# Whole-array products for the first attention groups, and the conversion's shifted words in one PSUM bank

## The chip, the cores and the metric

The kernel runs on one core of one Trainium2 chip. The metric is the device time of one execution in microseconds (us). Engines: PE (TensorE), DVE (VectorE), ACT (ScalarE), POOL (GpSimd), and SP, which here only issues DMAs. Matrix products take their operands from SBUF and write to PSUM, which has eight banks; a bank holds 512 fp32 words per partition.

## The reference

Windowed attention, then two feed-forward stages on its output. q and k are drawn with larger factors than v; the weights w1, w2, w3, w_out, w_in and w_out2 are float64.

```python
def _attn_ref(q, k, v):                       # (4, 8, 576, 64)
    window = 64
    scores = 1.0 / np.sqrt(D) * np.matmul(q, k.transpose(0, 1, 3, 2))
    rel = pos[:, None] - pos[None, :]
    scores = np.where((rel >= 0) & (rel < window), scores, -1000000000.0)
    scores = scores - np.max(scores, axis=-1, keepdims=True)
    attn = np.exp(scores)
    attn = attn / (np.sum(attn, axis=-1, keepdims=True) + 1e-09)
    return np.matmul(attn, v)

def _moe_ref(x, w1, w2, w3, w_out):           # x: 2304 x 512, d_ff 1024
    return ((x @ w1) * (x @ w2) @ w3) @ w_out

def _moe2_ref(x, w_in, w_out):                # d_ff 2048
    h = x @ w_in
    return (h * (1.0 / (1.0 + np.exp(-h)))) @ w_out
```

## The kernel before

**Weights.** They come as 64-bit words and are made into fp32 on the chip, 72 chunks of 128x512. A chunk (class `Chunk`) is loaded by SP (`words`), then ACT takes the scaled upper halves into `cv_b` and the lower halves into `cv_r` (L106, L107), DVE shifts `cv_b` by three bits in place (L115, `fraction`), DVE puts the sign bit of the upper half back (L118, `sign`, inputs `words` and `cv_b`), and POOL adds the rounded lower half (L122). Most chunks are then split into a high and a low part for three-pass products: ACT makes the high part (L130), DVE or POOL the low part (L134). `steps_to` runs this as a pipeline of chunk steps; the DVE steps of a chunk wait in `parts` and are put between the attention's DVE steps by `fill`.

**Attention.** 72 groups g of 128 queries and two heads. The first 17 (`PLAIN`) are computed in plain fp32, whose product of one instruction in the program is two records on PE; the others with split operands. `half` 2g transposes the probabilities of group g-1 (L286), computes the scores of g (L242; on 64 rows of the array, one product a head) and lets DVE reduce them with the mask (L253) and ACT exponentiate them; half 2g+1 normalises (L272, L274, L276 on DVE) and computes the values of g-1 (L311 and L312; each head in its own 64 columns of the array), which ACT copies out (L313).

**Stages.** The W stage (`phase_w`) multiplies w3 with w_out (L451, `accw`, in plain fp32), with 28 of the halves and the first conversions between its products. Then six blocks of phase A follow (`phase_a`, L479 and L499), which carry the other halves; block 0 has the rest of the first conversions, the last block those of w_in and w_out2 (`hooks5`). The last stage computes `h` (L601), its gate (ACT L606, DVE L607, ACT and POOL L79, L82) and `o` (L620), and the last conversions run on into its first rows. All instructions stand in the order in which the code issues them; each engine and SP works its list off in that order and waits at semaphores.

**PSUM.** Pool `ps` has four banks under one tag that rotate for the sums accw, ab, x and h; `psa` has one bank for scores, one for transposes and two for values.

Of the kernel before, what the change touches and what calls it, by code (L numbers as in the profile page):

```python
# [22 lines left out]
NB = 384  # L23
# [18 lines left out]
@with_exitstack  # L42
def tile_window_attention_ffn(ctx, tc, qkv, mask, ident, w1, w2, w3t, w_out, w_in, w_out2, out):

# [7 lines left out]
    main = ctx.enter_context(tc.tile_pool(name="main", bufs=1))  # L52
    ps = ctx.enter_context(tc.tile_pool(name="ps", bufs=4, space=PSUM))
    dram = ctx.enter_context(tc.tile_pool(name="dram", bufs=1, space=DRAM))
# [21 lines left out]
    def split(hi, lo, src, eng_hi, eng_lo):  # L76
# [7 lines left out]
        )  # L84

    PASSES = ((0, 0), (0, 1), (1, 0))


    class Chunk:
# [19 lines left out]
        def stage1(self):  # L109


            b = self.b

            def fraction():
                nc.vector.tensor_scalar(out=b, in0=b, scalar1=3, scalar2=None, op0=ALU.logical_shift_left)  # L115

            def sign():
                nc.vector.scalar_tensor_tensor(  # L118
                    out=b, in0=self.high, scalar=-0x80000000, in1=b, op0=ALU.bitwise_and, op1=ALU.bitwise_or
                )  # L120
# [62 lines left out]
    sm = [att.tile([128, 2, 192], F32, name=f"sm{i}", tag=f"sm{i}", bufs=1) for i in range(2)]  # L183
    k_lo = [att.tile([128, 384], F32R, name=f"klo{i}", tag=f"klo{i}", bufs=1) for i in range(2)]
    HEADS = (0, slice(0, 64)), (1, slice(64, 128))
    xhl = {}
# [12 lines left out]
    def load_qk(g):  # L199
        if g < NG and g not in loaded:  # L200
            loaded.add(g)
            qk_raw[g] = att.tile([128, 768], F32, name=f"qk{g}", tag="qk", bufs=2)
            u, c = place(g)
            p, f = (slice(0, 64), slice(128, 768)) if plain(g) else (slice(0, 128), slice(0, 768))
            nc.sync.dma_start(out=qk_raw[g][p, f], in_=qkv[u, c, p, f])

    def load_v(g):
        if g < NG and ("v", g) not in loaded:
            loaded.add(("v", g))
            v_raw[g] = att.tile([128, 3, 64], F32, name=f"v{g}", tag="v", bufs=3)  # L210
            u, c = place(g)
            nc.sync.dma_start(out=v_raw[g].rearrange("p t d -> p (t d)"), in_=qkv[u, c, :, 768:960])
# [23 lines left out]
    def scores(g):  # L236
        s_ps = psa.tile([128, 2, 192], F32, name=f"s{g}", tag="s")
        t = qk_raw.pop(g) if plain(g) else qk_st.pop(g)
        n = 64 if plain(g) else 128
        for h in range(2):  # L240

            nc.tensor.matmul(  # L242
                s_ps[:, h], lhsT=t[0:n, 128 + h * 128 : 256 + h * 128], rhs=t[0:n, 384 + h * 192 : 576 + h * 192],
                start=(h == 0), stop=(plain(g) and h == 1),
            )
        if not plain(g):
            nc.tensor.matmul(s_ps, lhsT=t[:, 0:128], rhs=k_lo[g % 2], start=False, stop=True)  # L247
# [128 lines left out]
    def phase_w():  # L376
# [36 lines left out]
        ready += [W12_B + 24 + (4 if W12_B == 16 else 0)] * 2  # L413

        loads_to(2)
        load_qk(0)
# [9 lines left out]
        load_v(2)  # L426
        for t in k_lo:
            for h, hs in HEADS:
                nc.gpsimd.memset(f32(t[hs, 192 - h * 192 : 384 - h * 192]), 0.0)
        steps_to(ready[0])  # L430
# [4 lines left out]
        for s in range(16):  # L435
            sw, j = divmod(s, 8)
            loads_to(ready[s + 2] + (3 if s > 1 else 0))
            if j == 0:
                for i in range(4):
                    acc[i] = ps.tile([128, 512], F32, name=f"accw{sw}_{i}", tag="ps")  # L440
            for part in range(2):
# [19 lines left out]
    def phase_a(blk, hooks):  # L461
# [9 lines left out]
        for s in range(16):  # L471
            f, m = divmod(s, 2)
            unit(s)
            fs = slice((f % 4) * 128, (f % 4 + 1) * 128)
            acc = ps.tile([128, NB], F32, name=f"ab{blk}_{s}", tag="ps")
            for k in range(4):
# [12 lines left out]
        for o in range(4):  # L489
            acc = ps.tile([128, NB], F32, name=f"x2_{blk}_{o}", tag="ps")  # L490
            for f in range(8):
# [25 lines left out]
    with tc.manual_schedule():  # L517
# [4 lines left out]
        for blk in range(1, NBLK - 1):  # L522
            phase_a(blk, lambda n: None)
        late.close()


# [67 lines left out]
        def emit_h(j, f):  # L594
            x = x2t[j]
            n = x.shape[-1]
            acc = ps.tile([128, n], F32, name=f"h{j}_{f}", tag="ps")
            fs = slice((f % 4) * 128, (f % 4 + 1) * 128)
# [73 lines left out]


def masks():

# [38 lines left out]
```

## Time and profile before

| | us |
|---|---|
| median of 3 runs (lowest to highest) | 904.78 (904.33 to 905.51) |
| the profiled execution | 904.8 |
| its span, first to last instruction | 903.0 |
| busy: PE, DVE, ACT, POOL | 877.2, 517.6, 492.0, 437.4 |

The profiled execution has a time of its own, and its span leaves out what lies before its first and behind its last instruction. Busy times are sums over the whole span. PE is the busiest engine in all stages, and DVE is close to full in two of them only: up to some 110 us (W stage) and from some 460 to 570 us (last conversions). What a shorter DVE or PE step is worth must be read from these stages.

### The profile page before, as it was taken

Reading aid. Unit: us, or ns where it says so; the run is one execution under the profiler, and the core shown is the slowest. Engines: PE = TensorE matmul, PEld = TensorE weight load, DVE = VectorE, ACT = ScalarE, POOL = GpSimd, SP = SyncE. Lnnn points to the kernel's source line nnn. Section 1 sums busy time; section 2 is a strip of 40 time slices with the busy share of each in tenths; the row PEclk is TensorE's granted clock in tenths of the full one; section 3 lists DMA queues with packets and bytes.
Section 4 is the critical chain, followed back from the end, with each engine's and each line's share of the span. In section 5 each row is a group of like instructions: output and inputs, shape, how many; then the busy total and the mean of one; then the engine's idle time right before and its main releaser. Section 6 shows DMA issues by size and latency. Waiting matters only on the chain.

```text
span 903.0 us, 13301 instructions
## 1 busy us (share of the span) xinstructions
PE 877.2 (97%) x4430; PEld 741.9 (82%) x4430; DVE 517.6 (57%) x1202; ACT 492.0 (54%) x1219; POOL 437.4 (48%) x470
## 2 busy tenths in 40 slices
PE   5999899999999999999999999999999999999998
PEld 2444378999999999999998776788888888888896
DVE  6989777888888878878488899311111111111111
ACT  6676577787788778787475775322222222222222
POOL 4557546556555566456297668422322232223222
PEclk9999899999999999999999999999999999999999
DMA  8866413332333322431567500110011000100100
GB/s 291 282 220 225 121 51 95 113 114 89 115 101 106 115 97 89 125 109 49 187 227 275 221 0 1 48 47 0 1 47 47 1 0 24 47 1 0 48 1 24
DMA packets 39396, 84.71 MB, mean 94 GB/s; under 512 B 4320, under 2 KB 17632, under 8 KB 39328
## 3 DMA queue, kind: packets, MB, share of 16 engines
q1 hardware_dynamic: 33280, 74.43, 25.2%
q10 hardware_dynamic: 6048, 9.44, 2.8%
q8 instruction: 35, 0.57, 0.3%
q14 instruction: 33, 0.27, 0.1%
HBM read 74.42 MB, written 9.44 MB: 93 GB/s over the span
## 4 chain that ended last, share of the span: by engine, by line
PE 78%; DVE 9%; POOL 4%; DMA 4%; issue 3%; ACT 2%; SPq 1%; POOLq 0%; DVEq 0%; ACTq 0%
PE o L620 18%; PE h L601 18%; PE ab L479 18%; PE x L499 10%; DVE cv_b L115 3%; PE accw L451 3%; PE t L286 2%; DVE cv_b L118 2%; PE s L242 2%; PE o L318 2%; DVE hl L134 1%; POOL cv_b L122 1%; PE s L247 1%; DMA qk<-in_qkv 1%; PE o L319 1%
## 5 line engine op out<-in xcount | busy, mean ns | idle before, releaser
L620 PE MATMUL o<-hl,g 128*128 128x512 f32 x864 | 213.0, 392 | 4.1 <-POOL g L82 3.6
L601 PE MATMUL h<-x2t,hl 128*128 128x512 f32 (+1 forms) x960 | 213.4, 371 | 0.0
L82 POOL TENSOR_TENSOR g<-sg,g 128x512 fp32r<-128x512 f32 (+1 forms) x80 | 96.0, 1200 | 241.9 <-ACT g L79 227.4
L607 DVE TENSOR_TENSOR sg<-h,sg 128x512 f32<-128x512 f32 (+1 forms) x80 | 51.0, 637 | 279.7 <-ACT sg L606 279.7
L601 PEld LDWEIGHTS h<-x2t,hl 128*128 128x128 f32 x960 | 169.4, 188 | 33.9
L620 PEld LDWEIGHTS o<-hl,g 128*128 128x128 f32 x864 | 160.3, 188 | 42.0 <-POOL g L82 6.8
L606 ACT ACTIVATE sg<-h 128x512 f32<-128x512 f32 (+1 forms) x80 | 44.2, 553 | 187.7 <-PE h L601 187.7
L479 PE MATMUL ab<-xa,hl 128*128 128x384 f32 x576 | 116.6, 337 | 0.0
L479 PE MATMUL ab<-xb,hl 128*128 128x384 f32 x576 | 115.6, 335 | 0.0
L479 PEld LDWEIGHTS ab<-xb,hl 128*128 128x128 f32 x576 | 101.4, 188 | 0.0
L479 PEld LDWEIGHTS ab<-xa,hl 128*128 128x128 f32 x576 | 99.4, 188 | 0.9 <-issue 0.7
L122 POOL TENSOR_TENSOR cv_b<-cv_b,cv_r 128x512 int32<-128x512 int32 x48 | 74.0, 1542 | 43.5 <-DVE cv_b L118 35.3
L326 POOL TENSOR_TENSOR xr<-ot 128x128 f32<-128x128 f32 x55 | 33.1, 602 | 118.3 <-DVE ot L325 116.3
L79 ACT CAST g<-sg 128x512 fp32r<-128x512 f32 (+1 forms) x80 | 46.3, 579 | 72.2 <-DVE sg L607 72.2
L118 DVE SCALAR_TENSOR_TENSOR cv_b<-words,cv_b 128x512 int32<-128x512 int32 x72 | 77.4, 1076 | 2.0
L264 ACT ACTIVATE sm<-sm,nm 128x192 f32<-128x192 f32 x144 | 64.5, 449 | 23.6 <-DVE nm L253 22.2
L223 POOL TENSOR_TENSOR klo<-qk,qkhi 64x192 fp32r<-64x192 f32 x110 | 69.9, 635 | 7.1 <-ACT qkhi L219 2.9
L115 DVE TENSOR_SCALAR cv_b<-cv_b 128x512 int32<-128x512 int32 x72 | 64.5, 896 | 10.0 <-ACT cv_b L106 10.0
L499 PE MATMUL x<-p,wp 128*128 128x384 f32 x360 | 69.6, 335 | 0.0
L499 PEld LDWEIGHTS x<-p,wp 128*128 128x128 f32 x360 | 62.2, 188 | 0.1
L106 ACT ACTIVATE cv_b<-words 128x512 f32<-128x512 f32 x72 | 48.1, 668 | 17.3 <-POOL hl L134 7.3
L253 DVE CUSTOM_DVE_ANT_0 sm<-s,mask_sb 128x192 f32<-128x192 f32 x144 | 45.6, 354 | 7.4 <-PE s L242 4.5
(79 smaller groups left out, 1271.6 us busy)
## 6 DMA issues: line engine op xcount, KB each, us to landing
qk<-in_qkv SPq DMA_DIRECT2D x55, 384.0 KB, 3.1
words<-in_w_out SPq DMA_DIRECT2D x24, 512.0 KB, 8.1
words<-in_w3t SPq DMA_DIRECT2D x16, 512.0 KB, 6.0
words<-in_w SPq DMA_DIRECT2D x16, 512.0 KB, 6.0
words<-in_w_in SPq DMA_DIRECT2D x16, 512.0 KB, 7.0
v<-in_qkv SPq DMA_DIRECT2D x72, 96.0 KB, 2.6
x2d<-x2s ACTq DMA_DIRECT2D x24, 192.0 KB, 1.9
out_x<-osb ACTq DMA_DIRECT2D x18, 256.0 KB, 2.1
```

What stands on the lines that cost most here:

```text
L82: (nc.vector if eng_lo == "dve" else nc.gpsimd).tensor_tensor(out=lo, in0=src, in1=f32(hi), op=ALU.subtract)
L106: nc.scalar.activation(out=f32(self.b), in_=f32(self.high), func=AF.Copy, scale=2.0**-112)
L115: nc.vector.tensor_scalar(out=b, in0=b, scalar1=3, scalar2=None, op0=ALU.logical_shift_left)
L118: nc.vector.scalar_tensor_tensor(out=b, in0=self.high, scalar=-0x80000000, in1=b, op0=ALU.bitwise_and, op1=ALU.bitwise_or)
L122: nc.gpsimd.tensor_tensor(out=x, in0=b, in1=self.r, op=ALU.add)
L223: nc.gpsimd.tensor_tensor(out=k_lo[g % 2][hs, h * 192 : h * 192 + 192], in0=t[hs, n], in1=f32(hi[hs, n]), op=ALU.subtract)
L264: nc.scalar.activation(out=x, in_=x, func=AF.Exp, scale=-1.0, bias=nm[:, h : h + 1], accum_out=rs[:, h : h + 1])
L479: nc.tensor.matmul(acc, lhsT=w[:, l, fs], rhs=x[k // 2][:, k % 2, r, :], start=(k == 0 and n == 0), stop=(k == 3 and n == 2),)
L499: nc.tensor.matmul(acc, lhsT=wp[f][:, l, o * 128 : (o + 1) * 128], rhs=p[f][:, r, :], start=(f == 0 and n == 0), stop=(f == 7 and n == 2),)
L601: nc.tensor.matmul(acc, lhsT=weights["in", f // 4, k][:, l, fs], rhs=x[:, k, r, :], start=(k == 0 and i == 0), stop=(k == 3 and i == 2),)
L607: nc.vector.tensor_tensor(out=sg, in0=acc, in1=sg, op=ALU.mult)
L620: nc.tensor.matmul(oacc[t], lhsT=g[:, l, t * 128 : (t + 1) * 128], rhs=weights["out", f][:, r, :], start=(f == 0 and i == 0), stop=(f == 1 ...
```

## The change

**Plain groups.** Their queries are loaded as a 128x128 tile with both heads one above the other, and their keys into `k_p`, whose upper half holds head 0's 192 columns and whose lower half head 1's, with zeros elsewhere (cleared once by POOL). One product of 128 rows and 384 columns gives both heads' scores. Their values come from a new input array `vp`, 128x320 a group, packed on the host with zeros, so that three products on all 128 columns accumulate both heads' outputs. A group's loads are three DMAs for q and k and one for v, where there were one and one.

**Conversion.** The shift writes its result into a PSUM tile `z` (`cv_z` in the rows below) and the sign step reads it from there; its output goes to `cv_b` as before. One bank serves all chunks.

**PSUM.** The four rotating banks get a tag each (`accumulator`). In the W stage and block 0, `z` takes the second values bank, so the values have one; after the first conversions the values alternate between both again. From the last block of phase A until the last chunk, `z` takes the fourth of the rotating banks and three rotate.

The order of work on DVE, ACT and POOL stays the same but for four more clears at POOL's start. Below are parts of the lists as they stand, without row numbers. On PE, one group of the W stage; `o` are the values, `s` the scores, `accw` the W stage's sums, `vp` and `kp` the new tiles. Before:

```order
L311 MATMUL o_271<-pw_82,v_105 64x128
L312 MATMUL o_271<-pw_82,v_105 64x64
L311 MATMUL o_271<-pw_82,v_105 64x128
L312 MATMUL o_271<-pw_82,v_105 64x64
L451 MATMUL accw_0_145<-wo,q 128x512
L451 MATMUL accw_1_146<-wo,q 128x512
L286 MATMUL t_296<-id_sb,sm_72 128x128 x3
L242 MATMUL s_300<-qk_220 128x192 x2
```

and after:

```order
L335 MATMUL o_289<-pw_87,vp_79 128x128
L336 MATMUL o_289<-pw_87,vp_79 128x128
L337 MATMUL o_289<-pw_87,vp_79 128x64
L476 MATMUL accw_0_156<-wo,q 128x512
L476 MATMUL accw_1_157<-wo,q 128x512
L308 MATMUL t_315<-id_sb,sm_72 128x128 x3
L261 MATMUL s_319<-kp_77,qk_236 128x384
```

Four value products are three, two score products are one, and nothing moves past another. On DVE, the same group with the semaphores that each instruction waits for; `rs` and `sm` are the softmax's sums and rows. Before:

```order
L115 TENSOR_SCALAR cv_b<-cv_b 128x512 [waits Activation_49,Pool_49]
L272 TENSOR_SCALAR rs_189<-rs_189 128x2 [waits Activation_49]
L118 SCALAR_TENSOR_TENSOR cv_b<-words,cv_b 128x512 [waits DMAHW7_49,DVE_49]
L274 RECIPROCAL rs_189<-rs_189 128x2 [waits DVE_49]
L276 TENSOR_TENSOR sm_73<-sm_73,rs_189 128x384 [waits DVE_49]
```

and after:

```order
L125 TENSOR_SCALAR cv_z<-cv_b 128x512 [waits DVE_49,Activation_49]
L294 TENSOR_SCALAR rs_204<-rs_204 128x2 [waits Activation_49]
L128 SCALAR_TENSOR_TENSOR cv_b<-words,cv_z 128x512 [waits DMAHW3_49,DVE_49,Pool_49]
L296 RECIPROCAL rs_204<-rs_204 128x2 [waits DVE_49]
L298 TENSOR_TENSOR sm_73<-sm_73,rs_204 128x384 [waits DVE_49]
```

The shift (now L125) gains a wait for DVE's own earlier instruction, and the wait for POOL has gone from it to the sign step (now L128). On SP, early in the W stage; before:

```order
L205 DMA qk_220<-in_qkv 64x640
L212 DMA v_222<-in_qkv 128x192
L99 DMA words<-in_w_out 128x1024
L99 DMA words<-in_w3t 128x1024
L99 DMA words<-in_w_out 128x1024
```

and after:

```order
L219 DMA qk_236<-in_qkv 128x128
L223 DMA kp_77<-in_qkv 64x192 x2
L229 DMA vp_78<-in_vp 128x320
L107 DMA words<-in_w_out 128x1024
L107 DMA words<-in_w3t 128x1024
```

The words' loads stand behind two more DMAs in each group.

The diff's core:

```diff
-    ps = ctx.enter_context(tc.tile_pool(name="ps", bufs=4, space=PSUM))
+    ps = ctx.enter_context(tc.tile_pool(name="ps", bufs=1, space=PSUM))
...
+    turn = [0]
+    converting = {"z": lambda: psa.tile([128, 512], I32, name="cv_z", tag="z"), "banks": 4}
+    def accumulator(name, shape):
+        turn[0] = (turn[0] + 1) % converting["banks"]
+        return ps.tile(shape, F32, name=name, tag=f"ps{turn[0]}")
...
             def fraction():
-                nc.vector.tensor_scalar(out=b, in0=b, scalar1=3, scalar2=None, op0=ALU.logical_shift_left)
+                self.z = converting["z"]()
+                nc.vector.tensor_scalar(out=self.z, in0=b, scalar1=3, scalar2=None, op0=ALU.logical_shift_left)
             def sign():
                 nc.vector.scalar_tensor_tensor(
-                    out=b, in0=self.high, scalar=-0x80000000, in1=b, op0=ALU.bitwise_and, op1=ALU.bitwise_or
+                    out=b, in0=self.high, scalar=-0x80000000, in1=self.z, op0=ALU.bitwise_and, op1=ALU.bitwise_or
                 )
...
-            p, f = (slice(0, 64), slice(128, 768)) if plain(g) else (slice(0, 128), slice(0, 768))
-            nc.sync.dma_start(out=qk_raw[g][p, f], in_=qkv[u, c, p, f])
+            if not plain(g):
+                nc.sync.dma_start(out=qk_raw[g], in_=qkv[u, c, :, 0:768])
+                return
+            nc.sync.dma_start(out=qk_raw[g][:, 0:128], in_=qkv[u, c, :, 0:128])
+            for h, hs in HEADS:
+                n = slice(384 + h * 192, 576 + h * 192)
+                nc.sync.dma_start(out=k_p[g % 2][hs, h * 192 : h * 192 + 192], in_=qkv[u, c, hs, n])
...
+            if plain(g):
+                nc.sync.dma_start(out=v_p[g % 3], in_=vp[g])
+                return
...
+        if plain(g):
+            nc.tensor.matmul(s_ps, lhsT=t[:, 0:128], rhs=k_p[g % 2], start=True, stop=True)
...
-        o_ps = psa.tile([128, 2, 2, 128], F32, name=f"o{g}", tag="o", bufs=2)
+        tag = "z" if done["step"] == len(line) and g % 2 else "o"
+        o_ps = psa.tile([128, 2, 2, 128], F32, name=f"o{g}", tag=tag)
         if plain(g):
-            v, p = v_raw.pop(g), p_st.pop(g)
-            for h, hs in HEADS:
-                o = o_ps[hs, 0, 0]
-                nc.tensor.matmul(o, lhsT=v[:, h], rhs=p[:, h * 128 : h * 128 + 128], start=True, stop=False)
-                nc.tensor.matmul(o[:, 0:64], lhsT=v[hs, 2], rhs=p[hs, 256:320], start=False, stop=True)
-            nc.scalar.copy(out=xr[:, c, r : r + 128], in_=o_ps[:, 0, 0])
+            v, p, o = v_p[g % 3], p_st.pop(g), o_ps[:, 0, 0]
+            nc.tensor.matmul(o, lhsT=v[:, 0:128], rhs=p[:, 0:128], start=True, stop=False)
+            nc.tensor.matmul(o, lhsT=v[:, 64:192], rhs=p[:, 128:256], start=False, stop=False)
+            nc.tensor.matmul(o[:, 0:64], lhsT=v[:, 192:320], rhs=p[:, 256:320], start=False, stop=True)
+            nc.scalar.copy(out=xr[:, c, r : r + 128], in_=o)
...
+        for t in k_p + [f32(t) for t in k_lo]:
+            for h, hs in HEADS:
+                nc.gpsimd.memset(t[hs, 192 - h * 192 : 384 - h * 192], 0.0)
...
         late.close()
+        converting.update(z=lambda: ps.tile([128, 512], I32, name="cv_z", tag="ps3"), banks=3)
...
+                if j:
+                    converting["banks"] = 4
```

The sums' tiles (accw, ab, x2, h) are all taken through `accumulator`. The scratch memory for DMA descriptors that are made at run time is set to 1024 bytes.

## Rows read from the trace of the kernel before

**Rows 1.** The page's span, and its busy times of the engines
```profile
span 903.0 us, 13301 instructions
...
PE 877.2 (97%) x4430; PEld 741.9 (82%) x4430; DVE 517.6 (57%) x1202; ACT 492.0 (54%) x1219; POOL 437.4 (48%) x470
```

**Rows 2.** Stretches: length, busy (x count) PE, PEld, DVE, ACT, POOL, PEclk, DMA, GB/s
```profile
20.00:40.00 20.00, 19.57 (x69) 9.24 (x67) 19.72 (x39) 14.01 (x36) 11.19 (x8) 1.00 0.91 302
40.00:80.00 40.00, 38.59 (x139) 18.88 (x139) 35.43 (x70) 27.27 (x66) 25.81 (x19) 1.00 0.67 212
80.00:100.00 20.00, 15.76 (x50) 7.71 (x49) 19.30 (x33) 12.97 (x33) 14.41 (x10) 0.89 0.54 175
100.00:116.29 16.29, 16.29 (x53) 7.43 (x51) 9.43 (x23) 8.62 (x20) 6.35 (x8) 0.93 0.32 97
116.29:140.00 23.71, 23.36 (x131) 19.44 (x130) 18.68 (x43) 15.88 (x42) 13.04 (x11) 1.00 0.22 65
```

**Rows 3.** Groups by line, 19.7:110, then 480:567 (busy us, mean ns)
```profile
L118 DVE SCALAR_TENSOR_TENSOR cv_b<-words,cv_b 128x512 int32<-128x512 int32 x30 | 29.2, 972 | 0.6
L115 DVE TENSOR_SCALAR cv_b<-cv_b 128x512 int32<-128x512 int32 x30 | 26.0, 867 | 0.0
...
L118 DVE SCALAR_TENSOR_TENSOR cv_b<-words,cv_b 128x512 int32<-128x512 int32 x24 | 28.6, 1191 | 0.8
L115 DVE TENSOR_SCALAR cv_b<-cv_b 128x512 int32<-128x512 int32 x24 | 25.1, 1047 | 2.9 <-ACT cv_b L106 2.9
```

**Rows 4.** Timeline of PE, one plain group: start us, busy us, line, xrecords
```profile
21.52 0.49 PE L286 MATMUL t<-id_sb,sm 128*128 128x128 f32 x3
21.95 0.92 PE L242 MATMUL s<-qk 64*128 64x192 f32 x4
22.79 1.98 PE L451 MATMUL accw<-wo,q 128*128 128x512 f32 x4
24.70 0.43 PE L311 MATMUL o<-pw,v 128*64 128x128 f32 x2
...
25.32 0.43 PE L311 MATMUL o<-pw,v 128*64 128x128 f32 x2
...
25.94 1.98 PE L451 MATMUL accw<-wo,q 128*128 128x512 f32 x4
```

**Rows 5.** Timeline of DVE and POOL: shifts, POOL's additions, and L607
```profile
118.80 0.42 DVE L115 TENSOR_SCALAR cv_b<-cv_b 128x512 int32<-128x512 int32 x1
...
528.66 1.68 POOL L122 TENSOR_TENSOR cv_b<-cv_b,cv_r 128x512 int32<-128x512 int32 x1 [0.63 <-DVE cv_b L118]
529.11 1.52 DVE L115 TENSOR_SCALAR cv_b<-cv_b 128x512 int32<-128x512 int32 x1
...
531.50 1.61 POOL L122 TENSOR_TENSOR cv_b<-cv_b,cv_r 128x512 int32<-128x512 int32 x1 [1.16 <-DVE cv_b L118]
531.87 0.69 DVE L607 TENSOR_TENSOR sg<-h,sg 128x512 f32<-128x512 f32 x1
```

**Rows 6.** Timeline of PE behind the hole in W ([idle before <-releaser])
```profile
96.21 0.87 PE L286 MATMUL t<-id_sb,sm 128*128 128x128 f32 x3 [3.77 <-ACT cv_r L107]
...
98.59 3.78 PE L451 MATMUL accw<-wo,w3x 128*128 128x512 f32 x4
```

**Rows 7.** Timeline of PE in the last conversions
```profile
502.75 2.93 PE L601 MATMUL h<-x2t,hl 128*128 128x512 f32 x12
...
560.92 2.56 PE L620 MATMUL o<-hl,g 128*128 128x512 f32 x10 [2.21 <-POOL g L82]
...
569.50 2.98 PE L601 MATMUL h<-x2t,hl 128*128 128x512 f32 x12
...
575.08 2.98 PE L601 MATMUL h<-x2t,hl 128*128 128x512 f32 x12
```

**Rows 8.** Timeline of PE and DVE in the last block of phase A
```profile
462.90 0.54 DVE L487 TENSOR_TENSOR a<-ab,a 128x384 f32<-128x384 f32 x1
...
463.50 1.20 PE L479 MATMUL ab<-xa,hl 128*128 128x384 f32 x6
```

More of the change, by code (lines that the diff above doesn't have):

```diff
@@ L42, in tile_window_attention_ffn @@
 @with_exitstack
-def tile_window_attention_ffn(ctx, tc, qkv, mask, ident, w1, w2, w3t, w_out, w_in, w_out2, out):
+def tile_window_attention_ffn(ctx, tc, qkv, vp, mask, ident, w1, w2, w3t, w_out, w_in, w_out2, out):
     nc = tc.nc
     main = ctx.enter_context(tc.tile_pool(name="main", bufs=1))
-    ps = ctx.enter_context(tc.tile_pool(name="ps", bufs=4, space=PSUM))
+    ps = ctx.enter_context(tc.tile_pool(name="ps", bufs=1, space=PSUM))
     dram = ctx.enter_context(tc.tile_pool(name="dram", bufs=1, space=DRAM))
@@ L184, in tile_window_attention_ffn @@
     k_lo = [att.tile([128, 384], F32R, name=f"klo{i}", tag=f"klo{i}", bufs=1) for i in range(2)]
+    k_p = [att.tile([128, 384], F32, name=f"kp{i}", tag=f"kp{i}", bufs=1) for i in range(2)]
+    v_p = [att.tile([128, 320], F32, name=f"vp{i}", tag=f"vp{i}", bufs=1) for i in range(3)]
     HEADS = (0, slice(0, 64)), (1, slice(64, 128))
@@ L238, in scores @@
         t = qk_raw.pop(g) if plain(g) else qk_st.pop(g)
[L239 to L246, printed above, removed]
+        if plain(g):
+            nc.tensor.matmul(s_ps, lhsT=t[:, 0:128], rhs=k_p[g % 2], start=True, stop=True)
+        else:
+            for h in range(2):
+                nc.tensor.matmul(
+                    s_ps[:, h], lhsT=t[:, 128 + h * 128 : 256 + h * 128],
+                    rhs=t[:, 384 + h * 192 : 576 + h * 192], start=(h == 0), stop=False,
+                )
             nc.tensor.matmul(s_ps, lhsT=t[:, 0:128], rhs=k_lo[g % 2], start=False, stop=True)
@@ L426, in phase_w @@
         load_v(2)
-        for t in k_lo:
-            for h, hs in HEADS:
-                nc.gpsimd.memset(f32(t[hs, 192 - h * 192 : 384 - h * 192]), 0.0)
         steps_to(ready[0])
@@ L439, in phase_w @@
                 for i in range(4):
-                    acc[i] = ps.tile([128, 512], F32, name=f"accw{sw}_{i}", tag="ps")
+                    acc[i] = accumulator(f"accw{sw}_{i}", [128, 512])
             for part in range(2):
@@ L474, in phase_a @@
             fs = slice((f % 4) * 128, (f % 4 + 1) * 128)
-            acc = ps.tile([128, NB], F32, name=f"ab{blk}_{s}", tag="ps")
+            acc = accumulator(f"ab{blk}_{s}", [128, NB])
             for k in range(4):
@@ L489, in phase_a @@
         for o in range(4):
-            acc = ps.tile([128, NB], F32, name=f"x2_{blk}_{o}", tag="ps")
+            acc = accumulator(f"x2_{blk}_{o}", [128, NB])
             for f in range(8):
@@ L596, in emit_h @@
             n = x.shape[-1]
-            acc = ps.tile([128, n], F32, name=f"h{j}_{f}", tag="ps")
+            acc = accumulator(f"h{j}_{f}", [128, n])
             fs = slice((f % 4) * 128, (f % 4 + 1) * 128)
@@ L671, in packed_qkv, with plain_values @@
     return g
+def plain_values(qkv):
+    v = np.zeros((PLAIN, 128, 320), np.float32)
+    for g in range(PLAIN):
+        blk, r = divmod(g, 3 * NPAIR)
+        x = qkv[blk * 3 + r % 3, r // 3, :, 768:960]
+        v[g, :, 0:64], v[g, :, 128:192] = x[:, 0:64], x[:, 64:128]
+        v[g, 0:64, 192:256], v[g, 64:128, 256:320] = x[0:64, 128:192], x[64:128, 128:192]
+    return v
 def masks():
@@ L688 @@
     from concourse.bass_utils import run_bass_kernel_spmd
+    qkv = packed_qkv(inputs["q"], inputs["k"], inputs["v"])
     arrays = {
-        "qkv": packed_qkv(inputs["q"], inputs["k"], inputs["v"]),
+        "qkv": qkv,
+        "vp": plain_values(qkv),
         "mask": masks(),
@@ L703 @@
     arrays = {n: a.view(np.uint64) if a.dtype == np.float64 else a for n, a in arrays.items()}
-    nc = bacc.Bacc("TRN2", target_bir_lowering=False, num_devices=1)
+    nc = bacc.Bacc("TRN2", target_bir_lowering=False, num_devices=1, dynamic_dma_scratch_size=1024)
     args = {
```

## The prediction

> **What bounds the kernel now.** I read the page's first two parts first: TensorE (PE) is busy in 97% of a span of 903.0 us [rows 1]. So only stretches where PE idles, runs at the lower clock, or does work that can be made shorter can give time back. The table of stretches comes second [rows 2]: between 20 and 116.29 us PE is idle 0.43 + 1.41 + 4.24 + 0 = 6.1 us, and VectorE (DVE) is busy 19.72 + 35.43 + 19.30 + 9.43 = 83.9 of the 96.3 us. Two nearly full engines feed each other there. The large hole is at 92 to 96 us: PE stands 3.77 us, and behind it the next products run at half the clock (granted clock 0.89 and 0.93 of 2.4 GHz in these two stretches): the transposes take 0.87 us and four accw records 3.78 [rows 6], against 0.49 and 1.98 elsewhere [rows 4]; with the scores between them, 0.92 there, grown at the same factor, that is 2.9 us more. So 9.0 of the 96.3 us are lost and 87.3 are work of PE.
>
> Third, the reason why DVE is full. The conversion's shift (L115) takes 0.42 us when it meets no addition of GpSimd (POOL) and 1.52 us when it starts 0.45 us into an addition of POOL [rows 5]: it ends 0.29 us after POOL does, so it waited for it. Its mean is 867 ns in the W stage and 1047 ns in the last conversions; that of the sign step (L118) 972 and 1191 ns [rows 3]. L607, as long an operation with one input in PSUM, takes its usual 0.69 us in the middle of a POOL addition [rows 5]. Fourth, the end of the conversions: from 502.75 to 575.08 us there are 12 intervals from one h product to the next, 72.3 us in all, and the last, undisturbed one takes 5.58 [rows 7]. 12 of those are 67.0, so 5.4 us are lost; the largest single piece is a wait of 2.21 us for POOL's g.
>
> **The change part by part.** *Full-array products, PE.* Of a plain group, the scores now are four records of 64x192, 21.95 to 22.79 = 0.84 us, and the values eight records on 64 columns, 24.70 to 25.94 = 1.24 us [rows 4]. After the change the scores are two records with 384 columns on the whole array. The accw rows are such records with 512 columns, 1.91 us for four from start to start: 0.48 each, and by columns 0.36, so 0.72; by bare streaming, no more than 192 columns cost now, it could stay at 0.84. I take 0.70, a gain of 0.14 (0 to 0.16). The values are six records, four of 128 columns and two of 64. The nearest row is the transposes, three full-array records of 128 columns in 0.43 us up to the next start, 0.143 each [rows 4]: 4 x 0.143 + 2 x 0.07 = 0.71, at most 6 x 0.143 = 0.86. I take 0.71, a gain of 0.53 (0.38 to 0.58). Times 17 groups, 0.67 each: 11.4 us of PE. In the W stage lie 13 value steps and 14 score steps, 6.9 + 2.0 = 8.9 us; the rest, 2.5 us, falls into the first block of phase A, where PE idles only 0.35 us in 23.71 [rows 2], so it counts in full.
>
> What could speak against it: the old products of the two heads stand in different halves of the array's columns. In the trace the second head's value step starts 0.62 us after the first's, 25.32 against 24.70, once both of its products have begun [rows 4]; they do not overlap, so nothing is lost by joining them. The Trainium skill (TensorE: Matmul & The Clock Gate, "Part 3: Packing small matmuls") has small products on different tiles run at the same time, which would make the split form the better one; were that so here, the old value step would cost about half, the gain of 0.53 would be gone, and the sum would come out some 7 us higher. The trace disagrees, as the products are issued here.
>
> *The shifted words in PSUM, DVE.* L115 gets a PSUM output and L118 a PSUM input. No row of before has DVE write PSUM. Below it is bounded by the 0.42 us of its free SBUF form, above by its worst row, 1.52; the nearest row is L607, the same size with one PSUM operand, 0.69 [rows 5], and I take 0.65. L118 then is L607's like, 0.69. Both lose the wait for POOL. The page VectorE: DVE Perf Modes of the Trainium skill ("Why PSUM operands drop a tier") says that a PSUM operand takes fp32 operations out of the double-rate form, so it speaks against this edit: the unobstructed shift should rise from the 0.42 of the trace to about the 0.69 of L607; by that the sum would be 0.7 us higher than with my 0.65.
>
> The pair goes from 1.84 us in W to 1.34, and from 2.24 at the end to 1.34. But with one bank z, each shift now also waits for the sign step before it (the added wait for DVE in the order), where today the two overlap: I charge 0.1 us per pair. Behind a waiting shift stand the softmax steps of the group, for which ScalarE and then PE's transposes wait. And POOL, never stopped by these two steps any more, is more often running when the remaining steps that share with it come (L272, the normalising product L276, the low parts): up to 0.4 us for each of 13 groups, 5 us. In the W stage: 30 x (1.84 - 1.34 - 0.1) = 12 us, less 3 of those 5, is 9 us of DVE: 83.9 becomes 75.
>
> *What of it reaches the end.* W stage from 20 us on: PE's work is 87.3 - 8.9 = 78.4, DVE's 75. Today the sum of both, 171.2, takes 96.3 us, a ratio of 1.78. The two shrink alike, so I keep that ratio: 153.4/1.78 = 86.2, **10 us less**. Bounds: with the 9.0 us of losses down to 2, 80.4, a gain of 16; with DVE's part hidden, 4. Block 0 of phase A: **2.5 us** less. The last conversions: DVE's pairs shed 24 x 0.8 = 19 us in a stretch where 5.4 are lost, POOL's additions no longer wait for them, and PE becomes the bound; I count **4.5 us** less (1 to 6).
>
> *Edits that I cost at little.* The query, key and value loads of a plain group: three DMAs instead of one for q and k (the same 160 KB), v grows from 96 to 160 KB. SP is issued past the word loads in the same places, two issues later each group. In 20 to 40 us the DMA share is already 0.91 at 302 GB/s [rows 2], and 64 KB at that rate are 0.2 us; for the first eight groups 1.7 us of transfer, of which I put **0.5 us** on the path, 0 to 3 if the shorter rows transfer badly. GpSimd's added clears lie ahead of its first conversion. One bank fewer for the o tiles in W costs nothing if ScalarE's copy is done before the next group's values, a whole group of PE work later; without that cover PE would wait for a copy of 128 columns, less than L607's 0.69 for 512. The three banks that rotate in the last block leave a product the time of two others until it must be read. The latest reader today ends at 463.44, and the third product after it, which would take its bank, starts at 463.50 [rows 8]: it just fits, and DVE gets faster; each 0.1 us later would cost PE 0.1 us.
>
> Sum on the profiled execution, 904.8 us, of which the span is 903.0 (the median of the three runs is 904.78): 904.8 - 10 - 2.5 - 4.5 + 0.5 = 888.3, so **888 us**.
>
> **The rivals.** *A, the feed stays the bound in W (loads, or DVE that only trades one wait for another).* For: DMA share 0.91 up to 40 us; the ratio of DVE busy stays near 0.87. Against: loads fall to 212 GB/s after 40 us [rows 2]. W then gives 4, block 0 2.5, the end 4.5, and the loads cost 1: 895 us.
>
> *B, the stall goes whole.* The hole of 3.77 us and the 2.9 us at half clock are one event, and it may vanish with its cause. W gives 16, the end 6, block 0 2.5: 880 us.
>
> *C, the change does not free DVE.* If an operation that writes PSUM from SBUF still stands aside for POOL, L115 stays at 0.87 to 1.05 and only L118 gains, part of which the wait for z takes back. Against: L607, which reads PSUM; but no row shows a write. W gives 4 through PE, block 0 2.5, the end 0, plus 0.5: 899 us.
>
> *D, slower.* The write into PSUM is itself long. L115 would have to pass about 1.2 us; at 1.52 in every pair (1.52 + 0.69 + 0.1 = 2.31 against 1.84) DVE gains 30 x 0.47 = 14 us in W, to 98, more than the stage takes now with its idle time; with as much idle as today (12 us) the stage takes 110, 14 us more, less what PE saved in block 0: 916 us. Against: a like operation reading PSUM costs 0.69.
>
> **How the numbers follow.** Forecast 0.55, A 0.18, B 0.15, C 0.07, D 0.05. The measurement tells 0.2%, 1.8 us, from no change. The range takes in the forecast's own spread (884 to 892), A with a margin and most of B: 879 to 897; D, C and the edge of B lie outside, some 0.2. Faster by over 0.2% are the forecast, A, B and most of C: 0.93; within 0.2%: 0.02; slower: D, 0.05.
>
> **What would show it right or wrong.** The shift at 0.6 to 0.7 us whatever POOL does, and the sign step at 0.69 with no row above 1; the value step of a plain group in 0.7 us, scores in 0.7; the first ab product at 105 to 107 us (now 116.29, an edge of the stretches in [rows 2]); no PE gap of more than 1 us after 20 us and no half clock there; h products 5.6 us apart from 505 on. It is wrong if the shift's mean is over 1 us, if L272's and the normalising product's means grow by more than 0.5 us, or if ScalarE waits for the words' DMAs after 20 us.

## The result, and the profile after

The changed kernel takes 883.34 us (median of 4 runs, 882.29 to 884.13), the kernel before beside it 905.14. The ratio is 0.9757, 95% interval 0.9741 to 0.9773: 2.4% faster. Forecast were 888 us in a range of 879 to 897. The profiled execution is one of 884.13 us. The top of its page answers [rows 1]: 20.7 us of span have gone, 21.2 of PE and 36.9 of DVE.

```profile
span 882.3 us, 13255 instructions
...
PE 856.0 (97%) x4362; PEld 737.0 (84%) x4362; DVE 480.7 (54%) x1202; ACT 491.0 (56%) x1219; POOL 430.6 (49%) x474
```

DVE's two conversion steps answer [rows 3]: groups by line in the W stage, then in the last conversions (busy us, mean ns). L125 is the shift, L128 the sign step; 0.683 to 0.687 us on average in both places (windows 19.7:105 and 475:545) where 0.87 to 1.19 stood, and over all 72 chunks no row is longer than 0.70.

```profile
L125 DVE TENSOR_SCALAR cv_z<-cv_b 128x512 int32<-128x512 int32 x30 | 20.6, 687 | 1.8 <-ACT cv_b L114 1.3
L128 DVE SCALAR_TENSOR_TENSOR cv_b<-words,cv_z 128x512 int32<-128x512 int32 x30 | 20.6, 685 | 1.8 <-issue 0.5
```

```profile
L128 DVE SCALAR_TENSOR_TENSOR cv_b<-words,cv_z 128x512 int32<-128x512 int32 x20 | 13.7, 687 | 0.8
L125 DVE TENSOR_SCALAR cv_z<-cv_b 128x512 int32<-128x512 int32 x20 | 13.7, 683 | 2.4 <-ACT cv_b L114 2.4
```

A plain group on PE answers [rows 4] (timeline: start us, busy us, line, xrecords).

```profile
25.08 0.81 PE L261 MATMUL s<-kp,qk 128*128 128x384 f32 x2
25.73 1.88 PE L476 MATMUL accw<-wo,q 128*128 128x512 f32 x4
27.45 0.38 PE L335 MATMUL o<-pw,vp 128*128 128x128 f32 x2
...
28.06 1.94 PE L476 MATMUL accw<-wo,q 128*128 128x512 f32 x4
29.83 0.49 PE L308 MATMUL t<-id_sb,sm 128*128 128x128 f32 x3
30.16 0.81 PE L261 MATMUL s<-kp,qk 128*128 128x384 f32 x2
30.81 1.88 PE L476 MATMUL accw<-wo,q 128*128 128x512 f32 x4
```

The scores take 25.08 to 25.73 = 0.65 us and the values 27.45 to 28.06 = 0.61. From one accw row ahead of the values to the next it is 25.73 to 30.81 = 5.08 us. The same work took 22.79 to 29.02 = 6.23 before; its rows up to 25.94 are in [rows 4], and the next group's accw row is this:

```profile
29.02 1.98 PE L451 MATMUL accw<-wo,q 128*128 128x512 f32 x4
```

So a group is 1.15 us shorter on PE, though the scores and values themselves give only 0.19 + 0.63 = 0.82; e9 and e10 below take up the rest.

The hole in front of [rows 6] is gone, but two smaller ones remain in the W stage, and after 20 us PE still has a stretch at 1.2 GHz (granted clock 0.66 on average from 20 to 25 us, 1.00 from 25 to 30), where four accw records take 3.31 us:

```profile
21.61 3.31 PE L476 MATMUL accw<-wo,q 128*128 128x512 f32 x4
...
69.87 0.52 PE L308 MATMUL t<-id_sb,sm 128*128 128x128 f32 x3 [2.46 <-ACT cv_b L114]
...
90.00 0.52 PE L308 MATMUL t<-id_sb,sm 128*128 128x128 f32 x3 [2.07 <-DVE sm L298]
```

In the last conversions the h products now follow each other without a wait (first and last of the 13 rows that answer [rows 7]; 12 intervals, 66.80 us, where 72.33 stood):

```profile
487.30 2.93 PE L627 MATMUL h<-x2t,hl 128*128 128x512 f32 x12
...
554.10 2.98 PE L627 MATMUL h<-x2t,hl 128*128 128x512 f32 x12
```

Cut at points that every version has, the four stretches of the program read as follows (us, from the starts of PE rows; "again" are second profiles of the same kernels).

| | fourth accw row starts | from it to the first ab | first ab to the last block's first | last block to h(0,0) | h(0,0) to the end of the span |
|---|---|---|---|---|---|
| before | 22.79 | 93.50 | 326.41 | 47.54 | 412.76 |
| before, again | 23.75 | 92.51 | 326.59 | 47.56 | 413.69 |
| after | 25.73 | 78.83 | 324.46 | 45.77 | 407.51 |
| after, again | 23.20 | 78.95 | 324.47 | 45.76 | 407.52 |
| e1, products alone | 25.36 | 87.67 | 325.76 | 47.55 | 414.06 |
| e2, PSUM alone | 25.55 | 83.82 | 326.80 | 45.76 | 407.27 |
| e3, both, z in SBUF | 24.09 | 90.32 | 326.07 | 47.45 | 414.07 |

### The profile page after: what moved, and what is told of

It reads as the page before. It is cut to its first block, busy times and chain, and to the rows that moved or that the text cites. A ratio compares the mean times of both kernels' runs of the same rounds, so it can differ in the third digit from the quotient of the medians.

```text
span 882.3 us, 13255 instructions
## 1 busy us (share of the span) xinstructions
PE 856.0 (97%) x4362; PEld 737.0 (84%) x4362; DVE 480.7 (54%) x1202; ACT 491.0 (56%) x1219; POOL 430.6 (49%) x474
## 4 chain that ended last, share of the span: by engine, by line
PE 86%; DVE 2%; POOL 1%; issue 1%; ACT 0%; DMA 0%; POOLq 0%; SPq 0%; DVEq 0%
PE h L627 23%; PE o L646 22%; PE ab L504 21%; PE x L524 11%; PE t L308 2%; PE o L343 2%; PE s L265 1%; PE s L269 1%; PE accw L476 1%; PE o L344 1%; POOL klo L244 1%; DVE cv_b L128 0%; DVE cv_z L125 0%; DVE rs L294 0%; PE s L261 0%
## 5 line engine op out<-in xcount | busy, mean ns | idle before, releaser
L125 DVE TENSOR_SCALAR cv_z<-cv_b 128x512 int32<-128x512 int32 x72 | 49.4, 686 | 17.0 <-ACT cv_b L114 16.6
L128 DVE SCALAR_TENSOR_TENSOR cv_b<-words,cv_z 128x512 int32<-128x512 int32 x72 | 49.4, 686 | 3.5 <-issue 0.5
```

What stands on the lines that cost most here:

```text
L125: nc.vector.tensor_scalar(out=self.z, in0=b, scalar1=3, scalar2=None, op0=ALU.logical_shift_left)
L128: nc.vector.scalar_tensor_tensor(out=b, in0=self.high, scalar=-0x80000000, in1=self.z, op0=ALU.bitwise_and, op1=ALU.bitwise_or)
```

## The experiments

Times are medians; each ratio is to runs of the kernel before in the same series, with its 95% interval.

**e1, the products without the PSUM bank.** Against the changed kernel:

```diff
-                self.z = converting["z"]()
-                nc.vector.tensor_scalar(out=self.z, in0=b, ...
+                nc.vector.tensor_scalar(out=b, in0=b, ...
-                    out=b, in0=self.high, ... in1=self.z, ...
+                    out=b, in0=self.high, ... in1=b, ...
-        o_ps = psa.tile(..., tag=tag)
+        o_ps = psa.tile(..., tag="o", bufs=2)
```

> The full-array products and their loads alone: shift and sign write the SBUF tile b in place, as before the change, and the attention's output keeps its two PSUM banks. Theory (each part pays in its own place): the groups are 0.82 us cheaper on TensorE, the start costs about 2.5 us, the 13 lock waits of VectorE at the end and in block 0 stay: first ab product 4 to 8 us earlier than 116.3, last-block rows unchanged, 896 to 901 us. Rival (the conversions on VectorE set the pace of the whole weights' stage): the products gain nothing, 904 to 908 us. Second rival (the products are all of it in the weights' stage): first ab product at 104.6, 893 to 895 us. Shift and sign have means near 0.97 and 0.87 us with maxima above 1.2 in all three.

901.85 us, ratio 0.9951 (0.9932 to 0.9971), between the theory's range and the first rival's. The first ab product is 3.3 us earlier, less than the 4 to 8 of the theory, which had already charged 2.5 us for a late start. The start of this execution is 2.6 us late indeed; from the fourth accw row on 5.3 us go, where 12 groups at 0.82 us are 9.8. The row of that stretch shows why there is not more (length, then busy and count of PE, PEld, DVE, ACT, POOL, the granted clock, DMA share, GB/s):

```profile
25.36:113.03 87.67, 74.02 (x250) 38.73 (x248) 81.80 (x155) 59.70 (x146) 55.75 (x43) 0.96 0.70 223
```

PE's work falls to 74.0 us, but DVE stays at 81.8 of 87.7: shift and sign keep means of 0.85 and 0.97 us (the expectation has the two interchanged). The last stretches are those of the kernel before row by row, the long wait of [rows 7] included; here the ten records behind it took 4.14 us, 2.56 there and 3.38 in the second profile of the kernel before, at a granted clock of 0.72, 1.00 and 0.76 around them; that is most of what separates the ends of these three (414.06, 412.76 and 413.69 us).

**e2, the PSUM bank without the products.** In the kernel before, with the banks as in the change:

```diff
-                nc.vector.tensor_scalar(out=b, in0=b, ...
+                self.z = converting["z"]()
+                nc.vector.tensor_scalar(out=self.z, in0=b, ...
-                    out=b, in0=self.high, ... in1=b, ...
+                    out=b, in0=self.high, ... in1=self.z, ...
```

> The shift through the PSUM bank alone: the attention's plain groups keep their two products per head and their loads. Theory: shift and sign stand at 0.69 us each without a wait, the end of the program gains the same 7.3 us as with the whole change and block 0 about 2, the weights' stage 3 to 6 us (the hole before 102 us goes, the groups keep their TensorE time); 888 to 893 us. Rival (VectorE alone sets the pace): the weights' stage gains all of its 11.7 or more, 882 to 885 us. Second rival (the weights' stage is bound by TensorE): it gains 0 to 2 there, 894 to 896 us.

888.63 us, ratio 0.9809 (0.9787 to 0.9830): four fifths of the gain. Both last stretches are as short as with the whole change, so all that the end gives comes from DVE. Block 0, where I expected about 2 us, gives nothing (326.80 us). In the W stage 8.7 to 9.7 us go, more than the 3 to 6 that I expected, and the row says what stops it then: PE, which is busy for 83.6 of 83.8 us at the full clock.

```profile
25.55:109.37 83.82, 83.64 (x297) 41.11 (x297) 69.73 (x156) 61.04 (x146) 52.46 (x42) 1.00 0.74 228
```

**e3, the whole change with `z` in SBUF.**

```diff
-    converting = {"z": lambda: psa.tile([128, 512], I32, name="cv_z", tag="z"), "banks": 4}
+    converting = {"z": lambda: slot("cv_z", "cv_b2", [512], I32), "banks": 4}
```

The rotation of the accumulators stays as in the change.

> The whole change, but the shifted words pass through one tile in SBUF in place of the PSUM bank. Theory (it is PSUM that frees VectorE from waiting for GpSimd): shift and sign wait for GpSimd again, means of 0.9 to 1.0 us with maxima above 1.2, and the time is that of the products alone within 2 us. Rival (what helps is that the shift no longer writes the tile it reads, or the rotation of the accumulators): shift at 0.4 to 0.7 without waits and 882 to 885 us.

904.04 us, ratio 0.9978 (0.9968 to 0.9988). The waits are all back (groups by line, W stage):

```profile
L128 DVE SCALAR_TENSOR_TENSOR cv_b<-words,cv_z 128x512 int32<-128x512 int32 x31 | 29.8, 962 | 1.9 <-issue 0.5
L125 DVE TENSOR_SCALAR cv_z<-cv_b 128x512 int32<-128x512 int32 x30 | 26.3, 876 | 0.5
```

So neither the separate tile nor the rotation of the banks helps, only PSUM. It came out 2.2 us above e1, just outside "within 2"; DVE is busy for 83.2 us of its W stage against 81.8 in e1, and what that difference is made of I did not follow.

That the steps wait for POOL's use of a common path to SBUF is also what the Trainium skill says (SBUF — State Buffer, "Who interferes with whom"): by it a VectorE instruction of one SBUF input outside the double-rate form doesn't contend with GpSimd, while one with two SBUF inputs contends with a GpSimd instruction that reads SBUF. The rows agree: each of the two steps has one SBUF input in the changed kernel and no row above 0.70 us; in e3 the sign step has two and the shift is in a form that can run at double rate (0.41 us in its shortest rows), and both have rows above 1.5 us.

**r_before and r_after, second profiles; e4, fewer and longer loads.** In e4 the host packs keys and queries of a plain group into rows of 1280 bytes:

```diff
-            nc.sync.dma_start(out=qk_raw[g][:, 0:128], in_=qkv[u, c, :, 0:128])
             for h, hs in HEADS:
-                n = slice(384 + h * 192, 576 + h * 192)
-                nc.sync.dma_start(out=k_p[g % 2][hs, h * 192 : h * 192 + 192], in_=qkv[u, c, hs, n])
+                nc.sync.dma_start(out=k_p[g % 2][hs, h * 192 : h * 192 + 320], in_=kq[g, hs])
```

> The whole change, with q and k of a plain group packed by the host into 1280-byte rows, so that two loads of 64 partitions replace three loads with rows of 512 and 768 bytes; bytes of q and k are the same (160 KB a group), the values' wide load stays. Theory (the number of loads and their short rows make the start 2 to 3 us later): the accw product that was at 22.79 before and 25.73 after comes at 23.5 to 25, 881 to 882.5 us. Rival (the 64 KB of zeros more per group of the values' load do it): that product stays at 25.3 to 26, 883 to 884 us.

> The kernel before once more, for a second profile of its start. If the start of the weights' stage is as regular as the rest, the fourth accw row begins at 22.3 to 23.3 us again, and what the other kernels lose there (25.4 to 25.7 in three of them, one of which has the old loads) is theirs; if it lies at 24 or later here, the words' transfers vary from run to run by the 2 to 3 us that I had put down to the new loads.

> The changed kernel once more, for a second profile of its start and as a standard for the next two. 883 us within 1; fourth accw row at 25 to 26.5 us if the new loads make the start late, at 22.5 to 24.5 if it is chance.

The change's first profile starts its fourth accw row 2.9 us later than the kernel before, and I put that down to the loads. That reading fell. e4's fourth accw row, at 24.82 us, lies where its theory had it (23.5 to 25), and r_before's, at 23.75, between its two cases; but e2, with the old loads, is as late as the change (25.55), the second profile of the changed kernel is as early as the old ones (23.20), and e4 at 882.58 us, ratio 0.9736 (0.9715 to 0.9757), can't be told from the changed kernel's second series, 882.26 us, 0.9752 (0.9739 to 0.9765). Rows of the two profiles of the changed kernel:

```profile
20.58 0.49 PE L335 MATMUL o<-pw,vp 128*128 128x128 f32 x2 [1.92 <-ACT pw L314]
```

```profile
19.73 0.49 PE L335 MATMUL o<-pw,vp 128*128 128x128 f32 x2 [1.59 <-ACT pw L314]
...
20.45 1.94 PE L476 MATMUL accw<-wo,q 128*128 128x512 f32 x4
```

With either set of loads the start of an execution varies by 2.5 us or more, with the arrival of the words (ACT waits for them in all of these profiles) and with the stretch at 1.2 GHz that stands behind some of these waits: behind the one of 1.92 us the four accw records take 3.31 us (the row at 21.61 above), behind the one of 1.59 us 1.94. What the new loads cost lies below that, and e8 comes back to it.

**e7, the row sums of the softmax in PSUM as well.** The step that adds 1e-9 to them (L294, 128x2) waits for POOL too: its rows in the changed kernel go from 0.15 to 1.27 us. In e7 its operand lies in unused columns of the scores' bank, where the reciprocal and the normalising product read it as well:

```diff
-        s_ps = psa.tile([128, 2, 192], F32, name=f"s{g}", tag="s")
+        s_all = psa.tile([128, 512], F32, name=f"s{g}", tag="s")
+        s_ps = s_all[:, 0:384].rearrange("p (h n) -> p h n", h=2)
-        rs = att.tile([128, 2], F32, name=f"rs{g}", tag="rs", bufs=2)
+        rs = s_all[:, 384:386]
```

> The changed kernel with the softmax's row sums in two unused columns of the scores' PSUM bank, so that the step that adds 1e-9 to them reads and writes PSUM; nothing else. Theory (a VectorE step with its data in PSUM doesn't stand aside for GpSimd): that step, 0.46 us in the mean in the weights' stage with single rows of 0.99 against 0.16 when undisturbed, stays under 0.3 in every row; VectorE gets 3 to 4 us back over 13 groups, the TensorE gaps of 2 us before the transposes shrink, first ab product 1.5 to 3 us earlier, 880 to 882 us. Rival (VectorE isn't the bound any more in this stage): the rows are short and the time stays within 0.7 us of the changed kernel's. Second rival (the wait moves on to another step): low parts or casts grow by as much.

880.23 us, ratio 0.9723 (0.9710 to 0.9737), against 0.9752 (0.9739 to 0.9765) of the changed kernel in the same series: 2.0 us faster than the changed kernel, the two intervals just apart. The step in the changed kernel, then here:

```profile
L294 DVE TENSOR_SCALAR rs<-rs 128x2 f32<-128x2 f32 x13 | 6.0, 458 | 1.9 <-ACT sm L286 1.9
```

```profile
L295 DVE TENSOR_SCALAR s<-s 128x2 f32<-128x2 f32 x13 | 2.1, 160 | 4.1 <-ACT sm L287 4.1
```

Its 13 rows of the W stage fall from 6.0 to 2.1 us, and none of all 72 is longer than 0.17. Of that 1.1 us reach the first ab product, counted from the fourth accw row, where I had 1.5 to 3. The largest gap hardly moves (2.12 us, before the transposes): there, I think, the group's reduction, exponentials and normalisation follow one another on DVE and ACT, each behind a conversion step in its queue; no run tests that.

**e8, e4 and e7 together.**

> The packed loads of e4_pack and the sums in PSUM of e7_sums together. Theory (both pay, in different places): 879 to 881 us, 1 to 2 below the better of the two. Rival (one bound, words' loads or ScalarE, takes over in the weights' stage): the same as e4_pack, 882 to 883 us.

880.47 us, ratio 0.9730 (0.9711 to 0.9748): no different from e7. So the medians show no gain from the packed loads, in e4 or here. The profiles leave some 1 us open: from the fourth accw row to the first ab product e4 takes 78.07 us, 0.8 less than the change, and e8 76.44, 1.3 less than e7 (77.75). Between 20 and 110 us ACT waits for words for 0.3 to 3.1 us in all in the kernels with new loads (1.7 in both profiles of the change, 0.3 in e4), but not at all in e8 and in the three profiles with the old loads.

**e9 and e10, one of the two products alone.** e9 is the changed kernel with the scores per head, e10 with the values per head, each with its old products and loads:

```diff
-            nc.tensor.matmul(s_ps, lhsT=t[:, 0:128], rhs=k_p[g % 2], start=True, stop=True)
+            for h in range(2):
+                nc.tensor.matmul(s_ps[:, h], lhsT=t[0:64, 128 + h * 128 : ...], rhs=t[0:64, 384 + h * 192 : ...], ...
```

```diff
-            nc.tensor.matmul(o, lhsT=v[:, 0:128], rhs=p[:, 0:128], start=True, stop=False)
...
+            for h, hs in HEADS:
+                nc.tensor.matmul(o[hs], lhsT=v[:, h * 64 : ...], rhs=p[:, h * 128 : ...], start=True, stop=False)
+                nc.tensor.matmul(o[hs, 0:64], lhsT=v[hs, 128:192], rhs=p[hs, 256:320], start=False, stop=True)
```

> The changed kernel with the plain groups' scores per head again (four records on 64 partitions, one load of q and k as before); the values' products stay on the full array. Theory (a step on part of the array also makes its neighbours longer, because the weight load next to it is not hidden): in an undisturbed plain group the values take 0.61 us, the four accw records ahead of them 1.72 (1.91 before the change), the transposes ahead of the scores 0.42 and the scores 0.84, a period of some 5.4 us (6.24 before, 5.08 with the whole change); 884 to 886 us. Rival (the neighbours got shorter through the loads or by DVE's pace): accw ahead of the values at 1.91 here too, a period of 5.6.

> The changed kernel with the plain groups' values per head again (eight records on 64 columns, the values' load with rows of 768 bytes as before); the scores stay on the full array. Theory: values 1.24 us, accw ahead of them 1.91, transposes ahead of the scores 0.33 in place of 0.42, scores 0.65, a period of some 5.95 us; 886.5 to 888.5 us. Rival (the scores' neighbours don't change): transposes at 0.42, a period of 6.05.

884.62 us, ratio 0.9771 (0.9751 to 0.9790), and 886.11 us, 0.9786 (0.9771 to 0.9802). One plain group of e9, then of e10, on PE:

```profile
25.16 1.98 PE L474 MATMUL accw<-wo,q 128*128 128x512 f32 x4
26.98 0.39 PE L333 MATMUL o<-pw,vp 128*128 128x128 f32 x2
...
27.59 1.94 PE L474 MATMUL accw<-wo,q 128*128 128x512 f32 x4
29.36 0.49 PE L306 MATMUL t<-id_sb,sm 128*128 128x128 f32 x3
29.78 0.91 PE L256 MATMUL s<-qk 64*128 64x192 f32 x4
30.63 1.98 PE L474 MATMUL accw<-wo,q 128*128 128x512 f32 x4
```

```profile
23.91 1.88 PE L479 MATMUL accw<-wo,q 128*128 128x512 f32 x4
25.72 0.43 PE L337 MATMUL o<-pw,vp 128*64 128x128 f32 x2
...
26.95 1.99 PE L479 MATMUL accw<-wo,q 128*128 128x512 f32 x4
28.77 0.49 PE L309 MATMUL t<-id_sb,sm 128*128 128x128 f32 x3
29.10 0.81 PE L262 MATMUL s<-kp,qk 128*128 128x384 f32 x2
29.75 1.88 PE L479 MATMUL accw<-wo,q 128*128 128x512 f32 x4
```

The period is 30.63 - 25.16 = 5.47 us in e9 and 29.75 - 23.91 = 5.84 in e10, nearer to the theory's 5.4 and 5.95 than to the rivals' 5.6 and 6.05. The time of e9 lies where I expected it, that of e10 0.4 us below its range. The accw records ahead of the values took 1.91 us between two per-head steps [rows 4], take 1.82 and 1.81 with one per-head neighbour, and 1.72 with none; I had expected 1.72 for e9 and 1.91 for e10 at once. The transposes ahead of the scores take 0.42 us in e9 and 0.33 in e10. The weight loads show what differs (timeline of PEld: in e10 before and behind a per-head value step, in the changed kernel before a joined one):

```profile
24.77 0.19 PEld L479 LDWEIGHTS accw<-wo,q 128*128 128x128 f32 x1 [0.24 <-issue]
25.72 0.19 PEld L337 LDWEIGHTS o<-pw,vp 128*64 128x64 f32 x2 [0.76 <-ACT sm L287]
...
26.95 0.30 PEld L479 LDWEIGHTS accw<-wo,q 128*128 128x128 f32 x2
```

```profile
26.59 0.19 PEld L476 LDWEIGHTS accw<-wo,q 128*128 128x128 f32 x1 [0.24 <-issue]
27.02 0.19 PEld L335 LDWEIGHTS o<-pw,vp 128*128 128x128 f32 x1 [0.24 <-ACT sm L286]
27.45 0.19 PEld L335 LDWEIGHTS o<-pw,vp 128*128 128x128 f32 x1 [0.24 <-issue]
```

A whole-array load behind a whole-array product starts 0.43 us ahead of its own product (27.02 for the values at 27.45), under the record that is still running. The load onto 64 columns starts only with its product, at 25.72, and so does the whole-array load behind the per-head step, at 26.95. It isn't ACT that holds the one at 25.72 back: ACT had finished `pw` at 24.06. The Trainium skill (TensorE: Matmul & The Clock Gate, "Part 3: Packing small matmuls") says that a weight load is pulled ahead of running products if it goes to other rows of the array or to the background weight buffer, and, of traces, that loads overlap running products only if they go to other rows. For whole-array loads these rows agree with the first and not with the second: the load at 27.02 covers the rows that are in use, and is hidden.

What such PE time is worth shows in the stretch from the fourth accw row to the first ab product:

| | length | PE busy | DVE busy |
|---|---|---|---|
| e2, none joined | 83.82 | 83.64 | 69.73 |
| e10, scores joined | 80.63 | 79.16 | 70.80 |
| e9, values joined | 79.47 | 75.26 | 71.17 |
| the change | 78.83 | 71.03 | 71.07 |

The first 4.5 us of PE work that go (e2 to e10) shorten the stage by 3.2 us, the last 4.2 (e9 to the change) by 0.6. These are single profiles; by the ratios, the step from e9 to the change is 1.3 to 1.7 us of the whole kernel, with intervals that overlap.

## Why the prediction was right, and where it was off

**The bound, and the wait for POOL: right, with the mechanism shown.** e1 to e3 take the change apart: only a PSUM operand frees the two steps. The shift at 0.685 us (0.65 taken) and the sign step at 0.686 (0.69) were nearly exact. The Trainium skill (VectorE: DVE Perf Modes, "Why PSUM operands drop a tier") says that an fp32 operation with a PSUM operand runs at the single rate. The trace agrees for this shift of 32-bit integers: 0.685 us, as long as L607's 0.69, where its undisturbed SBUF form took 0.42 [rows 5].

**The W stage: the term was mis-sized, 14.1 us for 10,** from the fourth accw row on (93.0 to 78.9, the means of two profiles each). I kept the stage at 1/1.78 of the sum of PE's work at the full clock and DVE's busy time, because the two shrink alike. That came out: with the busy times of both in this stretch the ratio is (86.86 + 80.55) / 92.51 = 1.81 in the second profile of before and (71.03 + 71.07) / 78.83 = 1.80 after. It is no law: where PE alone got shorter it is 1.73 and 1.78 (e3, e1), where DVE did 1.83 (e2), and 1.86 in e10. What failed is the input for PE. I counted 0.67 us a group, scores and values alone, of which the values were 0.10 too slow and the scores 0.05 (and 13 value and 14 score steps from 20 us on, where 12 and 13 start); the trace has 1.15, because the neighbours' weight loads are now hidden (e9, e10). Over the 12 groups of the stretch that is 13.8 us of PE in place of 8.0; from e2 to the change, both at the full clock, PE's busy time falls by 12.6. By the rule, the 4.6 to 5.8 us that I missed are 2.6 to 3.3 of the 4.1 us that the term was short; no run separates the rest. DVE's input was right: 9.5 to 10.6 us less busy in the two profiles of the change than in the second of before, 9 taken.

```profile
23.75:116.26 92.51, 86.86 (x297) 41.94 (x296) 80.55 (x157) 60.54 (x146) 56.15 (x43) 0.96 0.65 206
```

```profile
25.73:104.56 78.83, 71.03 (x250) 37.14 (x248) 71.07 (x155) 59.23 (x146) 52.43 (x42) 1.00 0.79 249
```

The parts nearly add: e1 takes 5.3 us from this stretch, e2 9.2, both 14.1. The medians add as well, 0.49% and 1.91% against 2.43% and 2.48%. By the means of two profiles each, the stretches sum to 14.1 + 2.0 + 7.5 = 23.6 us, less 1.2 by which these two executions of the change started late: 22.4, against 21.8 and 23.0 by the medians of the two series.

**Waits that move on: about the right size, partly in other steps.** I charged 3 us in W for later steps that would meet POOL more often, and named L272, the normalising product and the low parts. The 13 rows of the 128x2 step have a mean of 0.458 us, less than in the kernel before, and the normalising product stays at 0.56. The four low parts rise from 3.8 to 5.8 us, and so do four casts that I had not named, from 3.9 to 5.8 (4.9 in the second profile). Together these steps take 3.5 us more, 2.0 in the second profile. Before, then after:

```profile
L272 DVE TENSOR_SCALAR rs<-rs 128x2 f32<-128x2 f32 x13 | 6.4, 493 | 0.3 <-ACT sm L264 0.3
...
L134 DVE TENSOR_TENSOR hl<-cv_b,hl 128x512 fp32r<-128x512 f32 x4 | 3.8, 944 | 0.0
L81 DVE CAST xa<-xr 128x384 fp32r<-128x384 f32 x2 | 2.2, 1094 | 0.6 <-ACT xr L313 0.6
...
L81 DVE CAST xb<-xr 128x384 fp32r<-128x384 f32 x2 | 1.7, 855 | 2.0 <-ACT xr L313 2.0
```

```profile
L144 DVE TENSOR_TENSOR hl<-cv_b,hl 128x512 fp32r<-128x512 f32 x4 | 5.8, 1453 | 0.0
...
L81 DVE CAST xa<-xr 128x384 fp32r<-128x384 f32 x2 | 2.9, 1434 | 0.0
L81 DVE CAST xb<-xr 128x384 fp32r<-128x384 f32 x2 | 2.9, 1434 | 0.0
```

So the two conversion steps give back some 13 us in this stretch, and DVE as a whole 10.

**The loads: 0.5 us can't be refuted.** The fourth accw row starts at 22.79, 23.75 and 25.55 us with the old loads and at 25.73, 23.20, 25.36, 24.09 and 24.05 with the new ones (after, again, e1, e3, e7): the means are 0.5 apart, with a spread five times that.

**Block 0: 2.0 us for 2.5.** I put this down to PE's shorter products alone, counted in full. But e1, the products alone, gives only 0.7 us there and e2 nothing; the two together give 2.0, so the gain needs both. Even then PE waits once for the normalised rows:

```profile
122.71 0.52 PE L308 MATMUL t<-id_sb,sm 128*128 128x128 f32 x3 [1.03 <-DVE sm L298]
```

**The end: under-sized, 7.0 to 8.0 us for 4.5,** by the two profiles of before. Between the h products of [rows 7] 5.5 us went (72.33 to 66.80), all of the 5.4 that I had found lost there; from h(0,0) to the end it is 5.2, and 6.2 against the second profile. I had counted only part of them and gave no reason. The other 1.8 lie in the last block of phase A, which the sum left out: two waits for ACT and POOL behind its x products. The kernel before, e1 and e3 have them, the kernels with `z` in PSUM don't; the two are 1.24 of the 1.8 us. In e1:

```profile
476.48 0.44 PE L521 MATMUL x<-q,wp 128*128 128x384 f32 x1 [0.60 <-ACT q L79]
477.56 0.62 PE L521 MATMUL x<-q,wp 128*128 128x384 f32 x2 [0.64 <-POOL q L82]
```

**What I said would show it.** Held: the shift and sign rows, values and scores (0.61 and 0.65 for 0.7), the first ab product (104.56 and 102.15 for 105 to 107: a little early), h products 5.57 apart from 487 on. Not held: "no PE gap of more than 1 us after 20 us and no half clock" - there are three of 2.46, 2.07 and, in block 0, 1.03 us, and the accw row at 21.61 stands at half clock. Of the signs of being wrong, the means of the shift, of L272 and of the normalising product stayed below their bounds, but the third came: ACT waits for a word load at 30.34 us (1.74 us), and in the second profile as well (1.4 and 0.3 us). By its own words the forecast would then have been wrong. The wait came, but the long stage that it was to announce did not, nor rival A's 895 us. Of the rivals, C and D fell with the first row of the shift. B's 880 us was nearer to the result than the forecast, but not by its mechanism alone: the hole went, while 7.8 us of PE idle time stayed in the stage. So the forecast was right in what it said would shorten the kernel and 4.7 us too high in the sum, mainly for two terms that were too small, W and the end.

## What to carry to other kernels

When two engines wait for each other's use of SBUF, pass an intermediate result through a free PSUM bank: it costs the undisturbed form some time (0.42 to 0.69 us here) and takes the wait away entirely, in the large steps first and then in the small ones (e7). When a product on part of the array is widened to the whole array, count its neighbours from start to start as well, since their weight loads move under running work. In a stage that two engines fill, the gains of both edits nearly added up here, while the last 4.2 us of PE work and the 3.9 us of DVE work in e7 were worth some 1 us each; and before a change is charged with a late start, profile both kernels twice.

## What the runs showed that I had not expected

- A partial-array step costs the accw records ahead of the values 0.09 to 0.1 us at each border (1.91, 1.82, 1.81 and 1.72 us with two, one, one and no such neighbours) and those behind the values 0.05 (1.82 against 1.77); the steps next to the products make 0.33 of the 1.15 us that a group gained.
- An add over 128x2 elements takes 0.15 to 0.17 us undisturbed and up to 1.27 when POOL is at work; with its data in PSUM its mean in the W stage is 0.160.
- Two profiles of the changed kernel differ by 2.5 us at its fourth accw row and agree within 0.2 us in every later stretch.
